# A fused Nystrom attention and squared-ReLU MLP kernel: the softmax A of batches 4 to 7 transposed by DMA instead of TensorE, with a gate on later loads and new instruction orders

## The chip, the cores and the metric

The kernel runs on one core of a Trainium2 chip. The metric is device microseconds of one execution (us). Medians are over the executions of a kernel; "span" is the length of the profiled execution, which is about 2 us shorter than the time reported for it.

## The reference, cut to what matters

```python
# per batch and head, S = 576, D = 64, m = 32 landmarks
A  = softmax(q    @ k_lm.T / 8)        # 576 x 32
Bm = softmax(q_lm @ k_lm.T / 8)        # 32 x 32
C  = softmax(q_lm @ k.T    / 8)        # 32 x 576
Z  = Bm.T / (norm1(Bm) * norminf(Bm) + 1e-6)
for _ in range(6):
    Z = 2 * Z - Z @ Bm @ Z             # the iterated inverse, a serial chain
attn = A @ Z @ C @ v
# then an MLP on 4608 rows: x (4608 x 512), w_in (512 x 2048), w_out (2048 x 512)
out = maximum(x @ w_in, 0) ** 2 @ w_out
```

There are 8 batches of 8 heads. The kernel folds Z @ C @ v @ w_in into a matrix G, so that the MLP's first product is h = G applied to A transposed (AT).

## The kernel before: the parts that matter

The order of instructions on TensorE, VectorE (DVE), ScalarE (ACT) and SyncE (SP) is written out by hand, in strings. `HEAD` orders batch 0's attention. `PLANS[b]` interleaves the MLP of batch b with the attention of batch b+1: `h` is one group of first products (4 matmuls), `s` its squaring on DVE, a number is so many steps of the output product (one 128x512 matmul each), `as`, `ar` are the sums and the scaling of A's rows, `at` its transpose, `gg` a part of G. `LOADS` orders the first loads.

```python
DMA_T = 3      # from this batch on q and k are transposed by DMA
DMA_A = 9      # the same for A: never, there are 8 batches
...
        def a_transposed(i):
            if b >= DMA_A:
                nc.sync.dma_start_transpose(AT[:, i, :]..., an[:, i, :, :]...)
                return
            tps = ntile([P, (NC4 + 1) * P], BF16, placed=b > 0)
            for c in range(NC4 + 1):                       # five 128x128 transposes on TensorE
                nc.tensor.transpose(tps[:, c * P:c * P + P], an[:, i, c, :], ident_bf[:])
            o = TAIL * c0
            return AT[:, i, o:o + S], tps[:, o:o + S]      # then one copy, DVE (i=0) or ACT (i=1)
...
    def mlp_in(b, f, AT, G, gT):
        h = psum.tile([P, 2, 512], F32, tag="h", bufs=2, name="h")
        for qd, j in order:
            nc.tensor.matmul(h[:, j, 0:HALF], lhsT=G[:, qd, f * P:(f + 1) * P],
                             rhs=AT[:, qd, a0 + j * HALF:a0 + (j + 1) * HALF], ...)
        r = mlp.tile([P, S], BF16, tag="r", bufs=3, name="r")
        nc.scalar.activation(r..., h[:, :, 0:HALF], AF.Relu)
        return lambda: nc.vector.tensor_tensor(gT[:, f, o:o + S], r[:], r[:], ALU.mult)
...
                if b > 0 and nm + "turn" in loaded[b - 1]:   # a load waits for the turning
                    tc.add_manual_dep(one.ins, loaded[b - 1][nm + "turn"].ins.name, ...)
```

`w:n:width` in `HEAD` is a filler: n matmuls whose result nobody reads.

The softmax here doesn't subtract the row's maximum and nothing guards it: scores larger than these inputs give would overflow.

Of the kernel before, what the change touches and what calls it, by code (L numbers as in the profile page):

```python
# [9 lines left out]
P = 128  # L10
# [19 lines left out]
HALF = S // 2  # L30
SCALE = 1.0 / 8.0
DMA_T = 3
DMA_A = 9
DMA_C = 9
COMPACT = 1
HEAD = (
    "w:16 ck tk1 mk w:1:256 w:1:256 ek1d w:1:256 w:1 tk0 tt w:1 w:1 cq0 cq1 ek0a mq tq0 tq1 "
    "lm w:1 et w:1:256 w:1 eq0a w:1:256 tl eq1d ls sum:0:4:5 w:1 ib w:1 w:1:256 sq1 w:1:256 "
    "if sk1 sum:1:2:5 w:1:256 w:1 sum:1:0:2 jo w:1:256 w:1:256 rec:1 w:1:256 row:1:0:3 "
    "row:1:3:5 w:1:256 sk0 w:1 sq0 jo w:1:256 w:1:256 w:1 w:1:256 sum:0:2:4 sum:0:0:2 w:1 jo "  # L40
    "rec:0 cv:0 cv:1 w:1:256 w:1:256 row:0:3:5 cr jo w:1:256 row:0:0:3 w:1:256 at:1 cba w:1 "
    "jl at:0 ea0d ea1a ct w:1:256 nu w:1:256 g:0 gl1d fv w:1 gf1d w:1 gf0a az gl0d"
)
LOADS = "w10 v0 w00 q1 w01 w11 o0 o1 o2 o3 v1"
PLANS = [
    (
        "pk h g:1 tt h pq h s tk1 s h s h tq1 s tk0 h h mk s s mq tq0 h lm s g:2 g:3 ls sk0 s h "
        "h ib 1 h 1 s if tl h jo 1 sq0 s 1 jo s s 1 h jo 1 sq1 1 jl h 1 nu h s s h nn 2 sk1 nu s "
        "1 s 8 as0 1 ar0 as1 2 ar1 5 nn1 cv 4 wt at0 2 gg0 2 at1 2 gg1 1"
    ),  # L50
    (
        "2 pk 1 h h 1 mk pq s mq 1 s h tq0 lm h ls h tt tq1 3 tl 1 s 1 h ib 1 s if s sq1 2 s h "
        "jo 1 as1 sq0 1 h h s 1 as0 tk1 1 jo 1 s 4 tk0 2 jo 1 h 1 s h 1 pk+ 1 jl ar1 h sk0 1 s 1 "
        "s nu h s 1 sk1 s h h nn s cv nu h 3 nn1 at1 s 3 s wt 3 ar0 2 gg0 3 at0 1 gg1 pq+"
    ),
    (
        "5 mk h 1 h mq s 2 h 5 lm s 2 ls 1 sk1 2 ib 3 h h s sk0 s if 1 s h 2 h 1 jo s h tl 3 jo "
        "1 s 2 h jo 1 s 2 h 3 s sq0 s 1 jl pk+ 4 sq1 2 as0 nu 3 h 1 nn 2 as1 1 pq+ 1 nu 1 h 1 "
        "ar1 h 1 s s h 1 nn1 cv 1 h 2 ar0 1 s wt h 1 at0 2 gg1 1 s at1 1 s 2 gg0 1 s"
    ),  # L60
    (
        "mk 2 h 1 mq 7 h 2 s lm s 1 ls 1 h sq1 1 h h 1 ib 1 s if sk1 1 s h s 2 h jo 1 s 1 h s 1 "
        "jo 2 h 1 pk+ jo 1 tl s h 2 jl as1 sq0 1 s h 1 s h nu s 1 h sk0 s 1 ar1 4 as0 nn 1 ar0 2 "
        "h 3 cv 2 s h nu 4 s nn1 1 at1 1 h wt 2 s 3 s gg1 1 at0 4 gg0 4 pq+"
    ),
    (
        "2 mk h 2 mq 4 h lm 1 h 1 s ls 1 sk0 s ib s 3 h h if 3 tl s 2 h h s 1 s jo 2 h h 1 jo s "
        "1 sq0 s 2 h 1 jo 5 s 10 jl pk+ s 3 sq1 h nu 1 h 1 h 3 as0 sk1 s 1 h 1 as1 ar1 5 s nn cv "
        "nu pq+ 4 s 2 nn1 ar0 h s 4 wt h 2 at0 s 1 gg0 2 s 1 at1 1 gg1 2"
    ),  # L70
    (
        "3 mk mq 3 h lm 3 h h ls 1 s 1 s ib 2 sq1 h 2 if 1 sq0 3 jo h 1 sk0 s jo 2 s h jo tl 4 "
        "as1 1 h 1 jl s sk1 h 3 pk+ s 4 nu h 1 s 2 s 1 s 4 as0 h 1 ar1 nn s 2 ar0 h cv h nu h s "
        "1 s 1 nn1 h 2 h pq+ s wt h 2 at1 2 gg0 at0 5 s 3 s s gg1"
    ),
    (
        "mk 1 mq 3 h s lm 1 h 3 ls 2 h s 1 ib 2 h 1 if sq1 s h 1 s 3 sq0 2 s h 2 s 2 jo h tl 3 "
        "jo 1 h h as0 jo 3 s h 1 s jl 1 s sk1 4 nu 2 as1 h nn 1 h 1 sk0 2 ar0 nu 1 s s 3 h h 1 "
        "cv 2 nn1 s h s 1 at0 1 wt h 2 s 1 ar1 gg0 1 at1 2 s 1 gg1 4 s"
    ),  # L80
    (
        "h 7 h 6 s 1 h 6 h 1 s 2 h s 2 h 6 s 13 h 2 s 2 h 1 s 1 s 5 s h 3 h 1 s s h 11 s 1 h s 8 "
        "h 1 h 1 h 1 s 4 s h 2 s s"
    ),
]

# [2 lines left out]
def kernel(  # L89
# [9 lines left out]
    nc = tc.nc  # L99
# [27 lines left out]
        nc.vector.memzero(ect[:])  # L127
        ects.append(ect)

    behind, gate = [], []  # L130

    def load(dst, src, queue=nc.gpsimd):
        with tc.issue_after(behind[0].ins) if behind else nullcontext():
            d = queue.dma_start(dst, src)  # L134
        if gate:
            tc.add_manual_dep(
                d.ins, gate.pop().ins.name,
                mybir.DependencyInfo(mybir.DependencyClass.Sync, mybir.DependencyReason.DATA),
                reason="q first")
        if queue is nc.gpsimd:  # L140
            behind[:] = [d]
        return d

    def k_row(b):
        return TAIL if b % 2 == 0 else 0

    def q_row(b):
        return TAIL - k_row(b)
# [12 lines left out]
    def load_qk(b: int, X: dict):  # L161

        X["qkt"] = loads.tile([P, H, D], BF16, tag="qkt", name="qkt")

        def tails():
            for src, r0 in ((k, k_row(b)), (q, q_row(b))):
                load(X["qkt"][r0:r0 + TAIL, :, :],
                     src[b, :, NC4 * P:S, :].rearrange("h p d -> p h d"))

        if b > 0:  # L170
            tails()
        for nm, src in (("k", k), ("q", q)):
            if b < 3:
                X[nm + "raw"] = staged(b, nm)
            else:
                X[nm + "raw"] = loads.tile([P, H, NC4, D], BF16, tag="raw", name="raw")
            parts = ((0, H // 2), (H // 2, H)) if b == 0 and nm == "q" else ((0, H),)
            for lo, hi in parts:
                one = load(
                    X[nm + "raw"][:, lo:hi, :, :],  # L180
                    src[b, lo:hi, 0:NC4 * P, :].rearrange("h (p c) d -> p h c d", c=NC4),
                    nc.sync if b == 0 and nm == "k" else nc.gpsimd)
                if b > 0 and nm + "turn" in loaded[b - 1]:
                    tc.add_manual_dep(
                        one.ins, loaded[b - 1][nm + "turn"].ins.name,
                        mybir.DependencyInfo(mybir.DependencyClass.Sync,
                                             mybir.DependencyReason.DATA),
                        reason="behind the turning of the batch before")
            if b == 0 and nm == "k":
                tails()  # L190

# [10 lines left out]
    loaded = {b: {} for b in range(B)}  # L202
# [31 lines left out]
    for i in range(2):  # L234
        ct = const.tile([P, 2, NC4 + 1, P], BF16, name="ct%d" % i)
# [1 line left out]
        cts.append(ct)  # L237
    nc.vector.tensor_copy(seg[:, NC4 + 2, :], seg[:, NC4, :])

    def load_rest(after):  # L240

        def w_in(i, j):
            load(
                w_in_bf[64 * i:64 * i + 64, :, 1024 * j:1024 * j + 1024],
                moe_w_in[256 * i:256 * i + 256, 1024 * j:1024 * j + 1024].rearrange(
                    "(j d) f -> d j f", d=D),
            )

        def w_out(j):
            load(  # L250
                w_out_bf[:, 4 * j:4 * j + 4, :],
                moe_w_out[512 * j:512 * j + 512, :].rearrange("(ft fp) c -> fp ft c", fp=P),
            )

        behind[:] = [masked]
        for x in LOADS.split():
            i = int(x[1])
            if x[0] == "w":
                w_in(i, int(x[2]))
            elif x[0] == "o":  # L260
                w_out(i)
            else:
                (load_v if x[0] == "v" else load_qk)(i, loaded[i])

    turn = [0]
# [32 lines left out]
    def attention(b: int, R: dict):  # L298

        X = loaded[b]  # L300
        BD = bds[b % 2]
        ect = ects[b % 2]
        first = b == 0
# [193 lines left out]
        ct = cts[b % 2] if b >= DMA_C else None  # L497
        c0 = b % 2
        at = NC4 * (1 - c0)
# [10 lines left out]
        an = attn.tile([P, 2, NC4 + 1, P], BF16, tag="an", bufs=1, name="an")  # L510
        AT = attn.tile([P, 2, (NC4 + 1) * P], BF16, tag="AT", name="AT")
# [55 lines left out]
        one, two = slice(0, 1), slice(1, 2)  # L567
# [20 lines left out]

        def a_transposed(i):
            if b >= DMA_A:  # L590
                nc.sync.dma_start_transpose(AT[:, i, :].rearrange("p (c t) -> p c t", t=P),
                                            an[:, i, :, :].rearrange("p c x -> p (c x)"))
                return
            tps = ntile([P, (NC4 + 1) * P], BF16, placed=b > 0)
            for c in range(NC4 + 1):
                nc.tensor.transpose(tps[:, c * P:c * P + P], an[:, i, c, :], ident_bf[:])  # L596
            o = TAIL * c0
            return AT[:, i, o:o + S], tps[:, o:o + S]
# [42 lines left out]
        act, dve = nc.scalar.copy, nc.vector.tensor_copy  # L641
# [67 lines left out]
        def head_step(token):  # L709
            st = X["state"]  # L710
            name, *args = token.split(":")
            i = int(name[2]) if len(name) > 2 and name[2].isdigit() else 0
            n = [int(x) for x in args if x.isdigit()]
            on = [x for x in args if not x.isdigit()]
            if name == "ck":
                raw = natural(0, "k")
                dve(X["k"][:, 0:2], raw[:, 0:2])
                load_rest(act(X["k"][:, 2:4], raw[:, 2:4]))
                st["qraw"] = natural(0, "q")
                X["tT"] = attn.tile([P, NPAIR, P], BF16, tag="tT", name="tT")  # L720
            elif name[:2] == "cq":
# [62 lines left out]
            elif name == "az":  # L784
                AZ = attn.tile([P, 2, (NC4 + 1) * P], BF16, tag="AT", name="AZ")
                az = [psum.tile([P, 2, 512], F32, tag="h", bufs=2, name="az") for j in range(2)]
# [187 lines left out]
```

## Time and profile before

| | before |
|---|---|
| time, median | 263.62 us (263.31 to 264.01, 4 runs) |
| span | 262.1 us |
| TensorE busy | 254.6 us, 97% of the span |
| first h (start of the MLP) | 23.51 us |
| transposes of A on TensorE | 80 |

The lines that carry this are shown in the prediction below. Two habits of reading are used throughout. First, matmuls overlap in the pipeline, so their durations don't add up to time (a 512-column matmul is recorded with 379 ns on average, but follows the one before it after 216); the chain of work that ended last gives pitches, which do. Second, the end of each batch's plan can be found in that chain: it is marked by the second G group of the plan (plus the few output steps that the plan has behind it), so the time of each plan can be compared between kernels.

### The profile page before, as it was taken

How to read it: one execution, taken by the hardware profiler on the slowest of the kernel's cores; microseconds unless marked ns; L12 is line 12 of the kernel's file. 1: busy time of each engine (PE TensorE's matmuls, PEld its weight loads, DVE VectorE, ACT ScalarE, POOL GpSimd, SP SyncE). 2: the span in 40 equal slices, each digit the busy share in tenths (PEclk: the TensorE clock that was granted, in tenths of full speed). 3: DMA queues.
4: the chain of work that ended last, by engine and by line, in shares of the span. 5: the costliest groups of instructions: out<-in, count | busy, mean ns of one | idle time of the engine just before them, and what ended most of it. 6: DMA issues, size and time to landing. Idle time of an engine off the chain costs nothing.

```text
span 262.1 us, 6993 instructions
## 1 busy us (share of the span) xinstructions
PE 254.6 (97%) x2894; PEld 154.1 (59%) x2894; DVE 176.8 (67%) x488; ACT 158.4 (60%) x278; POOL 45.2 (17%) x70
## 2 busy tenths in 40 slices
PE   7899999999999999999999999999999999999994
PEld 2674765476746655666566565566566655555453
DVE  5798777789985888699757587689776783232000
ACT  1556985478755856687567556775777664364210
POOL 8934234120010503301005010600000000000000
PEclk9999999999999999999999999999999999999999
DMA  8999999999549999995759979699401112112122
GB/s 185 201 194 205 208 205 189 204 210 90 116 48 207 126 173 214 160 170 109 144 103 95 204 149 181 92 197 216 102 22 40 43 43 80 40 44 80 40 80 80
DMA packets 69791, 34.65 MB, mean 132 GB/s; under 512 B 37376, under 2 KB 64256, under 8 KB 69760
## 3 DMA queue, kind: packets, MB, share of 16 engines
q0 software_dynamic: 39808, 17.83, 56.8%
q1 hardware_dynamic: 24704, 7.08, 16.0%
q10 hardware_dynamic: 5248, 9.31, 11.0%
q8 instruction: 22, 0.36, 0.6%
q14 instruction: 9, 0.07, 0.1%
HBM read 36.70 MB, written 9.44 MB: 176 GB/s over the span
## 4 chain that ended last, share of the span: by engine, by line
PE 91%; DVE 4%; DMA 2%; ACT 1%; issue 1%; DVEq 0%
PE ops L851 25%; PE h L822 24%; PE n L851 22%; PE g L805 3%; PE n L530 3%; DMA stage<-in_k_dram 2%; PE n L342 2%; PE n L414 2%; PE n L596 2%; PE idle L295 2%; PE n L614 1%; PE n L313 1%; PE n L629 1%; ACT r L826 1%; PE n L558 1%; DVE gT L827 1%
## 5 line engine op out<-in xcount | busy, mean ns | idle before, releaser
L826 ACT ACTIVATE r<-h 128x576 bf16<-128x576 f32 x128 | 81.3, 652 | 45.9 <-PE h L822 34.1
L851 PE MATMUL ops<-w_out_bf,gT 128*128 128x512 bf16 (+1 forms) x320 | 81.7, 368 | 0.0
L851 PEld LDWEIGHTS <-gT 128*128 128x128 bf16 x592 | 53.2, 98 | 38.7 <-issue 4.2
L851 PE MATMUL n<-w_out_bf,gT 128*128 128x512 bf16 x272 | 74.5, 379 | 0.0
L827 DVE TENSOR_TENSOR gT<-r 128x576 bf16<-128x576 bf16 x128 | 54.9, 448 | 27.2 <-ACT r L826 27.0
L822 PE MATMUL h<-AT,G 128*128 128x288 bf16 x448 | 71.0, 286 | 0.0
L822 PEld LDWEIGHTS <-G 128*128 128x128 bf16 x512 | 47.7, 97 | 24.2 <-ACT AZ L795 0.7
L703 DVE CAST G<-g 128x1024 bf16<-128x1024 f32 x14 | 17.1, 1224 | 5.4 <-PE g L805 5.4
L862 ACT COPY o_sb<-ops 128x512 f32<-128x512 f32 (+1 forms) x19 | 10.9, 574 | 14.5 <-PE ops L851 14.5
L862 ACT COPY o_sb<-n 128x512 f32<-128x512 f32 x17 | 10.0, 587 | 12.9 <-PE n L851 12.8
L703 ACT CAST G<-g 128x1024 bf16<-128x1024 f32 x14 | 14.2, 1015 | 4.5 <-PE g L805 4.5
L295 PE MATMUL idle<-bd 128*128 128x512 bf16 (+1 forms) x51 | 13.3, 377 | 1.5 <-DVE bd L117 1.5
L530 PEld LDWEIGHTS <-T 128*128 128x128 bf16 x256 | 11.3, 98 | 4.2 <-issue 0.6
L134 POOL DMA_DIRECT2D raw<-in_k_dram x5 | 4.5, 891 | 52.2 <-DVE gT L827 25.5
L572 DVE TENSOR_REDUCE ra<-EA 128x20 f32<-128x640 f32 (+3 forms) x19 | 13.2, 703 | 0.3 <-ACT EA L560 0.3
L584 DVE TENSOR_TENSOR an<-EA,rra 128x640 bf16<-128x640 f32 (+2 forms) x18 | 13.2, 737 | 0.2
L530 PE MATMUL n<-bd,T 128*128 128x64 bf16 x256 | 12.7, 193 | 0.0
L535 ACT ACTIVATE EA<-n 128x512 f32<-128x512 f32 x16 | 9.6, 598 | 3.3 <-PE n L530 3.2
L535 ACT ACTIVATE EC<-n 128x512 bf16<-128x512 f32 x16 | 9.5, 596 | 3.0 <-PE n L530 1.6
L134 POOL DMA_DIRECT2D raw<-in_q_dram x5 | 4.4, 884 | 38.2 <-DVE rc L445 17.1
L414 PEld LDWEIGHTS <-ED 128*128 128x128 bf16 x72 | 6.8, 98 | 6.5 <-DVE EY L453 0.9
L822 PE MATMUL h<-AZ,G 128*128 128x288 bf16 x64 | 10.0, 286 | 0.6 <-DVE AZ L795 0.4
(144 smaller groups left out, 287.2 us busy)
## 6 DMA issues: line engine op xcount, KB each, us to landing
out_dram<-o_sb ACTq DMA_DIRECT2D x31, 256.0 KB, 3.4
vm<-in_v_dram POOLq DMA_DIRECT2D x8, 512.0 KB, 10.8
raw<-in_k_dram POOLq DMA_DIRECT2D x5, 512.0 KB, 6.4
raw<-in_q_dram POOLq DMA_DIRECT2D x5, 512.0 KB, 6.2
w_in_bf<-in_moe_w_in_dram POOLq DMA_DIRECT2D x4, 512.0 KB, 12.1
w_out_bf<-in_moe_w_out_dram POOLq DMA_DIRECT2D x4, 512.0 KB, 17.0
out_dram<-o_sb ACTq DMA_DIRECT2D x9, 128.0 KB, 2.4
stage<-in_k_dram SPq DMA_DIRECT2D x1, 1024.0 KB, 5.9
```

The costliest lines, as they stand in the source:

```text
L295: nc.tensor.matmul(idle[:, 0:width], lhsT=z[:, 0:P], rhs=z[:, 0:width], start=True, stop=True)
L414: nc.tensor.matmul(res[a:a + w, qd, :], lhsT=diagonal[a:a + w, qd, :], rhs=moving(qd)[a:a + w], start=True, stop=True)
L530: nc.tensor.matmul(sc[:, c, j, :, :], lhsT=X[nm + "T"][:, c, p, :], rhs=BD[:, 1 if nm == "q" else 0, p, 0:64], start=True, stop=True)
L535: nc.scalar.activation(dst, sc.rearrange("p c j i m -> p c (j i m)"), AF.Exp, scale=SCALE)
L572: nc.vector.reduce_sum(ra[:, quads, lo:hi, :], EA[:, quads, lo:hi, :].rearrange("p q c (h m) -> p q c h m", m=M), axis=AX.X)
L584: on.tensor_tensor(an[:, i, lo:hi, :].rearrange("p c (h m) -> p c h m", m=M), EA[:, i, lo:hi, :].rearrange("p c (h m) -> p c h m", m=M), r ...
L703: (act, dve)[n % 2](G[:, :, n * 512:n * 512 + 512], gg[:])
L822: nc.tensor.matmul(h[:, j, 0:HALF], lhsT=G[:, qd, f * P:(f + 1) * P], rhs=AT[:, qd, a0 + j * HALF:a0 + (j + 1) * HALF], start=(qd == 0), s ...
L826: nc.scalar.activation(r.rearrange("p (j t) -> p j t", j=2), h[:, :, 0:HALF], AF.Relu)
L827: return lambda: nc.vector.tensor_tensor(gT[:, f, o:o + S], r[:], r[:], ALU.mult)
L851: nc.tensor.matmul(ops, lhsT=gT[:, f, t * P:t * P + P], rhs=w_out_bf[:, f, i * n:i * n + n], start=(f == 0), stop=(f == NF - 1))
L862: nc.scalar.copy(o_h, ops)
```

## The change

Its intent: TensorE is the bound, so take the 40 transposes of A of batches 4 to 7 off it and let the DMA engines do them, keep big loads from running beside them, and search anew for orders that suit this. The cut diff leaves out a branch that was never taken and is removed.

```diff
-DMA_A = 9
+DMA_A = 4
 HEAD = ( ... )    # rewritten: 51 fillers become 29, both halves of k transposed before its means
-LOADS = "w10 v0 w00 q1 w01 w11 o0 o1 o2 o3 v1"
+LOADS = "v0 w10 w00 q1 w11 w01 o0 o1 v1 o2 o3"
 PLANS = [ ... ]   # all eight rewritten; batch 0's plan has 12 output steps instead of 38
...
-                if b > 0 and nm + "turn" in loaded[b - 1]:
-                    tc.add_manual_dep(one.ins, loaded[b - 1][nm + "turn"].ins.name, ...)
+                turns = [] if b == 0 else [loaded[b - 1].get(nm + "turn")]
+                if b > 1 and nm == "k":
+                    turns += loaded[b - 2].get("aturn", [])
+                for turn in turns:
+                    if turn is not None:
+                        tc.add_manual_dep(one.ins, turn.ins.name, ...)
...
             if b >= DMA_A:
-                nc.sync.dma_start_transpose(AT..., an...)
+                X.setdefault("aturn", []).append(nc.sync.dma_start_transpose(AT..., an...))
                 return
```

I call the three lines about `aturn` the gate: k of batch 6 is loaded only after A of batch 4 is transposed, k of 7 after A of 5. The loads are issued in order, so q and v behind k wait too.

## The prediction

> **What bounds the kernel now.** I read the shares of the span first, then the chain of work that ended last, then the busy time by stretch, then the groups split by shape.
>
> ```profile
> PE 254.6 (97%) x2894; PEld 154.1 (59%) x2894; DVE 176.8 (67%) x488; ACT 158.4 (60%) x278; POOL 45.2 (17%) x70
> ...
> PE 91%; DVE 4%; DMA 2%; ACT 1%; issue 1%; DVEq 0%
> ```
>
> TensorE is busy for 97% of the span and carries 91% of the chain that ended last; no other engine is above 67%. That busy share alone doesn't say that it runs at its rate, because matmuls overlap. So I take pitches from the chain, where each piece is the time until the next piece begins (columns: start us, length us, what):
>
> ```profile
> 19.63 0.28 PE n L596 x5
> ...
> 208.13 0.98 PE h L822 x8
> ...
> 248.07 3.45 PE n L851 x16
> ```
>
> One 512-column matmul takes 3.45/16 = 0.216 us of the engine, one 288-column matmul 0.98/8 = 0.123, one transpose of a 128x128 block of A 0.28/5 = 0.056, though the groups give means of 379, 286 and 219 ns. With such pitches I add up each batch's plan (16 groups h of 4 x 0.123, so many 512-column steps, the attention pieces of the next batch) and compare it with the distance between the ends of the plans, which the G groups (L805) mark in the chain. For the plans of batches 1 to 6 the sums are 24.9, 27.6, 27.0, 29.3, 26.3 and 26.5 us, the distances 25.4, 27.9, 27.3, 29.7, 27.2 and 26.9. **Only 0.3 to 0.9 us per batch is lost there**: in that part an instruction taken off TensorE is time off the kernel. Two parts lose more, and both are early:
>
> ```profile
> 0.00:24.00 24.00, 20.87 (x324) 12.92 (x324) 17.86 (x59) 10.74 (x21) 16.30 (x33) 1.00 1.26 195
> 24.00:48.00 24.00, 23.64 (x354) 15.03 (x353) 19.19 (x52) 17.45 (x33) 8.49 (x11) 1.00 1.35 201
> ...
> 187.00:213.00 26.00, 26.00 (x305) 15.94 (x303) 19.63 (x59) 17.33 (x31) 0.00 (x0) 1.00 0.17 50
> ```
>
> (columns: length, then busy time of PE, PEld, DVE, ACT, POOL with counts, clock, DMA share, GB/s). The head, from the landing of k at 6.7 to the first h at 23.51, is a serial chain for batch 0 with about 8.4 us of needed TensorE work in the 15.7 us from 7.82; the rest is filler matmuls ("idle", L295) and latency. The plan of batch 0, 23.5 to 51.8 = 28.3 us, has 24.9 us of TensorE work: 3.4 lost, while DVE and ACT are at 80% and 73% in that stretch.
>
> **What the Trainium skill says.** "TensorE: Matmul & The Clock Gate", section Back-to-back issue gap, gives a warm gap of N/2.4 + 2.5 ns for a single stream: 216 ns at 512 columns and 56 at 128. This trace agrees (216, 56). The same section's lower figure for a sustained stream, about 131 ns at 512, this trace does not show. The page's section on the HAM clock gate says that about 3.4 us of idleness halves the clock; the longest idle time of TensorE here is 1.5 us and the granted clock is 1.00, so fewer fillers should not cost clock. "DMA: Bandwidth & Descriptors", section Issuing engines are not separate DMA queues, says that transfers of SP, ACT and POOL share 16 engines and interleave. The trace agrees at least in that a raw load lands after 6.0 us at best and 16.5 at worst. "Perfetto Trace Analysis", section Identifying the Most-Contended Engine, warns of judging by matmul busy time; the 379 against 216 ns above is why I worked with pitches.
>
> **The change part by part.**
>
> 1. Removed: batches 4 to 7 no longer transpose A on TensorE. That is 4 batches x 2 halves x 5 = 40 transposes (80 to 40 in the order of instructions), 8 x 0.28 = **2.24 us of TensorE** on the path.
>
> ```profile
> L596 PE MATMUL n<-ident_bf,an 128*128 128x128 bf16 x80 | 7.1, 219 | 0.0
> ...
> L685 ACT COPY AT<-n 128x576 bf16<-128x576 bf16 x7 | 4.5, 644 | 1.2 <-PE n L596 1.1
> ...
> L685 DVE COPY AT<-n 128x576 bf16<-128x576 bf16 x7 | 3.2, 452 | 0.8 <-PE n L596 0.8
> ```
>
> Four copies of 0.64 us leave ACT (2.6 us) and four of 0.45 leave DVE (1.8 us). Neither is the bound there; I count nothing for it.
>
> 2. Added: 8 transposes by DMA of 128x640, issued from SP. The nearest measured thing is the transpose of the tail tT, 128x512:
>
> ```profile
> L286 SPq DMA_TRANSPOSE tT<-qkt x5: 1188/1244/1552, 54.5 to 161.5; - x5
> ...
> DMA to landing us min/median/max: 4.4/4.4/7.6
> ```
>
> So I estimate 1.4 us of SP each to issue and 4.5 us to land, some 6 us for the two of a batch after the later half of A is written. Is that hidden? From the later of the two row scalings (ar) to the first h that reads AT, I count TensorE pieces in the new plans: 11.6, 11.7, 9.3 and 8.8 us for batches 4 to 7. Take off about 2.3 us for DVE's lag and the 0.8 us scaling: 9.3, 9.4, 7.0 and 6.5 us are left for about 6. **Hidden, but in the last two batches by a hair to 1 us**; there the other DMA traffic is nearly over (50 GB/s in 187 to 213).
>
> 3. The new wait: k of batches 6 and 7 is loaded only after the transposes of A of batches 4 and 5. For batch 6 they land about 0.6 us after the plan of batch 4 begins; k then takes 0.9 to issue and 6.4 to land, q one issue more, so q is there at about 9; its cast stands some 11.5 us into that plan. For batch 7, k is there at about 7 and its cast stands at 9.5. About 2.5 us of slack each: no cost expected. Before, these k loads were issued at 122 and 155 us, long ahead of need.
>
> 4. Moved: the head. 51 fillers become 29 (7 fewer of 512 columns, 15 fewer of 256), and both halves of k are transposed before its means. Up to the softmax of the landmarks I find no gain: Eb has to wait behind a 1.0 us copy on ACT. After that DVE is what the steps of the inverse queue behind:
>
> ```profile
> 15.31 0.88 DVE L572 TENSOR_REDUCE ra<-EA 128x12 f32<-128x384 f32 x2
> 16.11 0.28 DVE L419 SCALAR_TENSOR_TENSOR EY<-EY,n 128x128 bf16<-128x128 bf16 x1
> ...
> 21.77 0.48 DVE L644 TENSOR_SCALAR G<-n,rc 128x256 bf16<-128x256 f32 x1 [0.59 <-PE n L805]
> 22.17 0.21 DVE L419 SCALAR_TENSOR_TENSOR v<-v,n 128x64 bf16<-128x64 bf16 x1
> ```
>
> The new order spreads sums and scalings differently (one sum ahead of the first step, the reciprocal and one sum behind it) and gives the first scaling of G that stood ahead of the last v to ACT. Walking both lists with these durations I get the last v at about 21.4 instead of 22.17 and the first h at about 22.6 instead of 23.51: **0.9 us**.
>
> 5. Moved: the plan of batch 0 now holds 12 output steps instead of 38, so 19.3 us of TensorE work, but its DVE list adds up to about 22 us and its ACT list to 21 at the pitches of the trace. It becomes bound by those two: some 23 us. Before, less the 26 steps moved out (5.6 us), it took 22.7. **Nothing gained, perhaps 0.3 lost.** Later plans get the steps (444 done by the end of batch 6's plan, 418 before) and run at TensorE's rate; from the one idle spot (0.4 us in batch 5's plan, 0.9 lost there) I credit 0.4.
>
> Sum: 2.24 + 0.9 - 0.3 + 0.4 = about 3.3 us, so 263.73 - 3.3 = **260.4 us** (1.3% faster).
>
> **Rivals.** (a) *The transposes or the gated loads come late*, and a wait for them takes the place of the 2.24 us. For it: the worst raw load took 16.5 us, transposes of T up to 8.8, and the DMA slices are at 9 tenths for much of 100 to 190 us. Against: the counts of slack above. It would show as TensorE or DVE idle on AT or raw and give 262 to 265. (b) *DVE and ACT become the bound in batch 0's plan* by more than I counted, since 26 output steps are gone from it and each h needs 0.65 us of ACT against 0.49 of TensorE; two bad us there give 262. (c) *The search found more than I see*: if the head falls to 13.5 us and batch 0's plan to its DVE sum, another 2 us go and 258.4 is reached. Against: the chain of the inverse keeps its steps. (d) *The removed transposes were hidden anyway*: against it, the sums of TensorE match the distances within 0.3 us in most batches.
>
> **Range and chances.** The first term is firm (2.24 us); the early terms are uncertain by about 1 us each, both ways, and rival (a) makes a tail to the slow side. 8 times in 10: 258.7 to 262.2. Faster by over 2% means under 258.5, which needs rival (c): 0.1. Slower by over 2% needs over 5 us of new waits: 0.02. Within 2%: 0.88.
>
> **What would show it.** Transposes at L596 at 40 with TensorE's busy time down; the plans of batches 3 to 6 (which hold the attention of batches 4 to 7) each 0.56 us shorter for the same number of steps; DMA transposes of AT landing in 4 to 6 us with no wait of TensorE for AT; no DVE wait for raw; first h at about 22.6; batch 0's plan about 23 us with DVE and ACT near full. A wait for AT or raw, a first h at 23.5 or later, or a batch 0 plan beyond 25 us would prove me wrong on that step.

## The result, and the profile after

| | before | after |
|---|---|---|
| time, median | 263.62 us (263.31 to 264.01, 4 runs) | 260.91 us (260.31 to 260.98, 4 runs) |
| span | 262.1 us | 258.8 us |
| transposes of A on TensorE | 80 | 40 |
| first h | 23.51 us | 21.99 us |

The ratio is 0.9891 (95% interval 0.9871 to 0.9912), so 1.1% faster, within the 2% that counts as the same.

From the page of the changed kernel (busy time, and the chain that ended last, by engine and line):

```profile
PE 250.1 (97%) x2832; PEld 150.7 (58%) x2832; DVE 174.9 (68%) x483; ACT 156.7 (61%) x275; POOL 45.5 (18%) x70
...
PE 86%; DMA 6%; POOL 4%; DVE 2%; issue 0%; ACT 0%; POOLq 0%; DVEq 0%
PE ops L852 26%; PE h L823 23%; PE n L852 23%; DMA stage<-in_q_dram 6%; PE g L806 3%; PE n L529 3%; PE n L341 2%; PE n L413 1%; PE n L614 1%; POOL qkt L134 1%; PE n L312 1%; PE n L629 1%; POOL stage L134 1%; PE n L596 1%; PE n L557 1%; POOL seg L205 1%
```

TensorE is still the bound, with 4.5 us less of busy time. New is what the 6% of DMA are: the landing of q of batch 1 (before, 2%, the landing of k of batch 0). The groups by shape, and the new transposes with their issues and landings:

```profile
L596 PE MATMUL n<-ident_bf,an 128*128 128x128 bf16 x40 | 3.7, 220 | 0.0
L685 ACT COPY AT<-n 128x576 bf16<-128x576 bf16 x3 | 1.9, 640 | 0.4 <-PE n L596 0.4
...
L685 DVE COPY AT<-n 128x576 bf16<-128x576 bf16 x3 | 1.4, 455 | 0.5 <-PE n L596 0.5
```

```profile
L590 SPq DMA_TRANSPOSE AT<-an x8: 1201/1382/2116, 127.8 to 213.7; - x8
...
DMA to landing us min/median/max: 2.6/3.9/4.7
```

They land in 3.9 us (the median; at most 4.7) and TensorE never waits for them. Now the time of each plan, from the marks in the chains. "Asked" is the difference of output steps times the 0.2156 us of one step; what is left is gained or lost otherwise.

| part | before, us (steps) | after, us (steps) | difference | asked by steps | left |
|---|---|---|---|---|---|
| start to first h | 23.51 | 21.99 | -1.52 | 0 | **-1.52** |
| plan of batch 0 | 28.31 (38) | 23.86 (12) | -4.45 | -5.61 | **+1.16** |
| batch 1 | 25.44 (46) | 29.85 (67) | +4.41 | +4.53 | -0.12 |
| batch 2 | 27.93 (68) | 29.88 (77) | +1.95 | +1.94 | +0.01 |
| batch 3 | 27.34 (65) | 27.81 (70) | +0.47 | +1.08 | **-0.61** |
| batch 4 | 29.68 (76) | 29.91 (79) | +0.23 | +0.65 | **-0.42** |
| batch 5 | 27.20 (62) | 27.17 (67) | -0.03 | +1.08 | **-1.11** |
| batch 6 | 26.87 (63) | 28.25 (72) | +1.38 | +1.94 | **-0.56** |
| batch 7, to the last output step | 42.21 (158) | 36.49 (132) | -5.72 | -5.61 | -0.11 |

The last column sums to -3.3 us, the difference of the spans (3.6 us follow the last output step in both). Plans 3 to 6, which hold the attention of batches 4 to 7, give 2.70 us: the 2.24 of the transposes and about 0.5 more in batch 5's plan, where a small idle time is gone. The head gave 1.5 us, but the plan of batch 0 took 1.2 of it back. Why is seen in two views of the changed kernel. The chain (start, length, what) and DVE's timeline, with what ended its idle time in brackets:

```profile
11.75 14.59 DMA stage<-in_q_dram
26.34 0.02 issue
26.36 0.70 DVE nat L280
```

```profile
23.32 0.69 DVE L280 COPY nat<-stage 128x2048 bf16<-128x2048 bf16 x1 [0.63 <-DMA stage<-in_k_dram]
...
26.36 0.69 DVE L280 COPY nat<-stage 128x2048 bf16<-128x2048 bf16 x1 [0.99 <-DMA stage<-in_q_dram]
```

DVE, ready earlier than before, now stands idle for k and q of batch 1 to land at 23.3 and 26.3 us. Before, it took q up at 25.6 with no wait:

```profile
25.63 0.68 DVE L281 COPY nat<-stage 128x2048 bf16<-128x2048 bf16 x1
```

And by stretches, the columns as in the prediction:

```profile
0.00:24.00 24.00, 20.11 (x318) 11.91 (x318) 17.69 (x60) 12.45 (x25) 16.23 (x33) 1.00 1.26 192
24.00:48.00 24.00, 22.77 (x374) 15.07 (x375) 21.19 (x55) 19.14 (x36) 8.91 (x12) 1.00 1.35 201
```

In 24 to 48 us DVE is now at 88% and ACT at 80%, and TensorE idles 1.2 us.

### The profile page after: what moved, and what is told of

The parts are those of the page before. It is cut to its first block, busy times and chain, and to the rows that moved or that the text cites. A ratio compares the mean times of both kernels' runs of the same rounds, so it can differ in the third digit from the quotient of the medians.

```text
span 258.8 us, 6890 instructions
## 1 busy us (share of the span) xinstructions
PE 250.1 (97%) x2832; PEld 150.7 (58%) x2832; DVE 174.9 (68%) x483; ACT 156.7 (61%) x275; POOL 45.5 (18%) x70
## 4 chain that ended last, share of the span: by engine, by line
PE 86%; DMA 6%; POOL 4%; DVE 2%; issue 0%; ACT 0%; POOLq 0%; DVEq 0%
PE ops L852 26%; PE h L823 23%; PE n L852 23%; DMA stage<-in_q_dram 6%; PE g L806 3%; PE n L529 3%; PE n L341 2%; PE n L413 1%; PE n L614 1%; POOL qkt L134 1%; PE n L312 1%; PE n L629 1%; POOL stage L134 1%; PE n L596 1%; PE n L557 1%; POOL seg L205 1%
## 5 line engine op out<-in xcount | busy, mean ns | idle before, releaser
L852 PE MATMUL n<-w_out_bf,gT 128*128 128x512 bf16 x272 | 72.1, 379 | 0.0
L134 POOL DMA_DIRECT2D raw<-in_k_dram x5 | 4.4, 888 | 80.3 <-DMA AT<-an 23.5
L294 PE MATMUL idle<-bd 128*128 128x512 bf16 (+1 forms) x29 | 9.3, 434 | 1.5 <-DVE bd L117 1.5
L341 PEld LDWEIGHTS <-nat 128*128 128x128 bf16 x256 | 8.2, 96 | 2.7 <-issue 0.5
```

The costliest lines, as they stand in the source:

```text
L134: d = queue.dma_start(dst, src)
L341: nc.tensor.matmul(means[:, ti, p, :], lhsT=src.rearrange("p h d -> p (h d)"), rhs=seg[:, c + (ti if c == NC4 else 0), :], start=(n == 0 a ...
L852: nc.tensor.matmul(ops, lhsT=gT[:, f, t * P:t * P + P], rhs=w_out_bf[:, f, i * n:i * n + n], start=(f == 0), stop=(f == NF - 1))
```

## The experiments

Twelve runs, of eleven kernels, were made, each of five rounds against the kernel before on the same chip; all gave correct results. Medians of the kernel before were 263.16, 263.61 and 263.50 us in the three sessions. Line numbers differ by a few between these kernels.

### What each of the two halves is worth alone

**1. New orders, A transposed on TensorE.**

```diff
 # changed kernel
-DMA_A = 4
+DMA_A = 9
```

> The changed kernel with its new orders and loads, but all of A transposed on TensorE again (and so no gate on k). Theory: the 40 transposes lie on TensorE's path, 8 x 0.28 = 2.24 us, so this takes 260.9 + 2.2 = 263.1 us (262.6 to 263.9, as the last copy of A of batch 7 may now be waited for). Rival, the transposes were hidden and the gain is all from the orders: 260.9 (260.5 to 261.4).

Measured: 264.06 us (262.99 to 265.94, 6 runs), ratio 1.0032 (1.0001 to 1.0062): no faster than the kernel before. (The interval just excludes 1, but three of the six executions, 262.99, 263.04 and 263.65, lie where the kernel before does.) The span of the profiled run is 261.9 us, 3.1 more than after; by the marks 1.47 us of it are in batch 3's plan, 0.71 in 4's, 0.55 in 5's, 0.28 in 6's. So the transposes do lie on TensorE's path (the rival fell), and under these orders they cost more than their 2.24 us. The excess is in batch 3's plan, 1.47 us for ten transposes of 0.56, where the second five wait for the copy of the first five:

```profile
127.49 0.45 PE L596 MATMUL n<-ident_bf,an 128*128 128x128 bf16 x5
127.78 0.38 PE L852 MATMUL n<-w_out_bf,gT 128*128 128x512 bf16 x1
128.62 0.44 PE L596 MATMUL n<-ident_bf,an 128*128 128x128 bf16 x5 [0.46 <-DVE AT L685]
```

The spread of 3 us was not expected; see experiment 11.

**2. Old orders, A transposed by DMA, no gate.**

```diff
 # kernel before
-DMA_A = 9
+DMA_A = 4
```

> The kernel before with its own orders and loads, and A of batches 4 to 7 transposed by DMA (no gate). Theory, the 2.24 us come from the transposes alone and the transfers are hidden under the old orders as well: 263.6 - 2.2 = 261.4 (261.0 to 261.9). Rival, the old orders leave AT no time to land: TensorE waits for AT and the time stays at 262.5 or more.

Measured: 267.24 us (267.10 to 267.93), ratio 1.0155 (1.0139 to 1.0170), slower by 1.6%. The rival holds, and more strongly than I had put it: TensorE waits 3.7 us for AT, 3.1 of it at batch 5's first h, and the granted clock is 0.66 in the 5 us from there on (166 to 171 us).

**3. Old orders with the gate as well.**

```diff
 # the changed kernel's code
-HEAD, LOADS, PLANS of the changed kernel
+HEAD, LOADS, PLANS of the kernel before
```

> The old head, loads and plans with the changed kernel's mechanism: A of batches 4 to 7 by DMA and the gate on k. Without the gate this took 267.2. Theory A, the gate is what makes the transposes land in time, whatever the orders: 261.4 (260.9 to 262.0), no wait of TensorE for AT. Theory B, the old orders issue a transpose too late for the next h even so, or the held k comes late for its cast: 263 or more, with a wait for AT or raw.

Measured: 265.14 us (264.63 to 267.66, 6 runs), ratio 1.0075 (1.0045 to 1.0106). By the two ratios, which are of two sessions, the gate takes back 2 us, but theory B holds. TensorE waits for AT twice: 1.8 us at batch 5's first h and 1.2 at batch 6's. The chain at the first:

```profile
159.62 1.02 ACT G L703
160.65 0.37 SPq L590
161.02 0.05 issue
161.07 5.24 DMA AT<-an
166.31 0.04 issue
166.35 0.42 PE h L823 x2
```

The old plan scales the second half of A at 157.4 us on DVE and wants it in h at 164.1. TensorE's own transposes could be slotted in between; the DMA transpose cannot: SP issues in order, and stands behind the transposes of q of batch 6 until 159.65, so those of A are issued from 159.8 and 161.1 us, and the second lands at 166.3. (The chain puts an issue down to ACT's G; on SP's timeline that issue begins at 159.82, before this G ends.) The new plan has the same transposes issued by 157.5 and its first h at 167.1. The gain therefore belongs to neither half: new orders alone 264.1, DMA alone 267.2 or 265.1, both together 260.6 to 260.9. The 3 us of spread in this run, at clocks of 0.997 to 1.00, are not explained.

### The gate

**4. The changed kernel without the gate.**

```diff
-                if b > 1 and nm == "k":
-                    turns += loaded[b - 2].get("aturn", [])
```

> The changed kernel with DMA transposes, but k of batches 6 and 7 no longer waits for the transposes of A of batches 4 and 5. Theory: the gate costs nothing and buys nothing that TensorE waits for: 260.9 (260.5 to 261.3); the transposes of AT may land later than 4.7 us, beside a raw load. Rival, the gate is needed, as loads slow the transposes until TensorE waits for AT: 262 or more with a wait on AT. Second rival, the gate holds k back in its own right: 260.3 or less.

Measured: 265.97 us (265.11 to 267.90, 6 runs), ratio 1.0115 (1.0081 to 1.0148). My theory fell and the first rival holds. POOL's timeline of this run: the loads of k and q of batch 6 and v of batch 5, issued from 126.4 to 129.8 us.

```profile
126.44 0.89 POOL L134 DMA_DIRECT2D raw<-in_k_dram  x1 [15.40 <-DVE ED L402]
127.31 0.90 POOL L134 DMA_DIRECT2D raw<-in_q_dram  x1
128.18 0.91 POOL L134 DMA_DIRECT2D vm<-in_v_dram  x1
```

SP issues the two transposes of A from 129.4 us on, just behind them. Their landing in this kernel, and what TensorE did:

```profile
DMA to landing us min/median/max: 2.6/4.4/12.6
```

```profile
139.68 0.41 PE L821 MATMUL h<-AT,G 128*128 128x288 bf16 x2 [0.51 <-DMA AT<-an]
143.49 0.64 PE L821 MATMUL h<-AT,G 128*128 128x288 bf16 x2 [3.40 <-DMA AT<-an]
```

A transpose that lands in at most 4.7 us with the gate took 12.6 behind 1.5 MB of loads (the two of batch 4: 10.2 and 12.6). Between the ends of plans 2 and 4 this run lost 5.5 us (64.3 against 58.8): 3.9 of waiting, the rest at a lowered clock after it (0.87 over 135 to 148 us). Another 1.6 us it lost in the head, which is no effect of the gate (experiment 11). In the changed kernel the same k load is issued at 132.9 us, after AT has landed, and no one waits for it; it is the only load that is seen to wait for AT there (23.5 us).

### The head and the first loads

**5. The changed kernel again**, as the measure for experiments 6 and 9.

> The changed kernel unaltered, as the measure for the runs beside it on the same chip. Both theories: 260.9 (260.3 to 261.2). If it shows the wide spread of the run with A on TensorE (263.0 to 265.9), the spread belongs to the thinner fillers of the head and not to that run's edit.

Measured: 260.63 us (260.55 to 260.76), ratio 0.9888 (0.9874 to 0.9903). No wide spread here; the same head shows one in experiments 8 and 10.

**6. The changed kernel with the head of before.**

```diff
-HEAD of the changed kernel
+HEAD of the kernel before
```

> The changed kernel with the head of before (51 fillers, first h at 23.5 in the old trace instead of 22.0). Theory: the chain of batch 1 hangs on the landing of its q (26.3 us), not on the first h, so of the head's 1.5 us only 0.4 us or less reaches the end: 261.3 (260.9 to 261.8). Rival: the head's gain goes through in full: 262.4 (262.0 to 262.9).

Measured: 261.03 us (260.70 to 261.39), ratio 0.9904 (0.9891 to 0.9917). First h is at 23.52 us instead of 21.99, and yet only 0.4 us is lost. The theory holds: DVE takes up q of batch 1 at 26.42 us here, without a wait, and at 26.36 in the changed kernel, after one. The chain runs through the head and the first h here, through q's landing there: all but 0.4 of the head's 1.5 us stop at that landing.

**7. The first loads in the old order**, v of batch 1 still early.

```diff
-LOADS = "v0 w10 w00 q1 w11 w01 o0 o1 v1 o2 o3"
+LOADS = "w10 v0 w00 q1 w01 w11 o0 o1 v1 o2 o3"
```

> The changed kernel with only the first six loads put back to the order of before (w10 v0 w00 q1 w01 w11; v1 stays ahead of o2 and o3). Theory: with the new order the two later quarters of w_in are issued together at 13.1 us and share the engines with q of batch 1, which lands at 26.3 instead of 25.0 us and starts the chain of batch 1 late; put back, q lands at about 25.0, the plan of batch 0 is up to 1.3 us shorter, and the kernel takes 260.0 (259.6 to 260.4). Rival, the plan of batch 0 is bound by the sums of DVE and ACT, whenever q lands: 260.9 (260.6 to 261.3).

Measured: 260.14 us (259.91 to 260.43), ratio 0.9883 (0.9867 to 0.9898), in a session where the kernel before took 263.16. The ratio is within the noise of the changed kernel's 0.9888 and 0.9891, so the time doesn't decide; the profile says more. There q is taken up at 25.45 instead of 26.36 us, and the stretch from first h to the second G group of batch 0's plan is 22.13 instead of 23.22 us, 1.1 of the up to 1.3 that were expected. But first h came at 22.53 instead of 21.99 (22.27 in the profiles of experiments 1 and 5, which have the new load order and the same head), so part of it was lost in the head. And q no longer sets the pace: DVE takes it up without a wait, and the chain runs through the first h.

```profile
25.45 0.69 DVE L280 COPY nat<-stage 128x2048 bf16<-128x2048 bf16 x1
```

From first h to that G group it is 22.1 us in each profile with the clock at 1.00 and either the old load order (experiments 7, 9 and the second of 10) or the old head (experiment 6); with the new head and the new load order it is 23.2, 22.7 and 22.7 (changed kernel, experiments 1 and 5). So the wait for batch 1's loads comes on top of some 22.1 us that stay. Of these DVE is busy 91% and ACT 85% in this run, so rival and theory each hold in part; no experiment shows that DVE and ACT are what the 22.1 us consist of.

**8. The same kernel once more.**

> The same kernel as the run with the six early loads in the old order, once more, beside the two that follow on one chip. If q of batch 1 sets the pace of batch 0's plan: 260.0 (0.6 to 0.9 under the changed kernel's 260.6 to 260.9). If the changed head loses as much as batch 0's plan gains: 260.5, within 0.3 of the changed kernel.

Measured: 259.50, 259.95, 260.50 in three executions, 262.49, 262.63 and 262.64 in three others; median 261.49, ratio 0.9915 (0.9876 to 0.9954). The faster three stand some 0.7 us below the changed kernel, the slower three show something else (experiment 11). What the old load order is worth in the time stays unresolved. In the profiles with the clock at 1.00 the second G group of batch 0's plan begins at 44.3 to 44.6 us with it (experiments 7, 9 and the second of 10, on TensorE's timeline), and at 45.0 to 45.1 with the new one (changed kernel, experiments 1 and 5): about half a microsecond.

### More batches

**9. Old load order, and A of batches 3 to 7 by DMA.**

```diff
-DMA_A = 4
+DMA_A = 3
-LOADS = "v0 w10 w00 q1 w11 w01 o0 o1 v1 o2 o3"
+LOADS = "w10 v0 w00 q1 w01 w11 o0 o1 v1 o2 o3"
```

> The changed kernel with the early loads in the old order (260.1 on its chip) and the A of batch 3 by DMA as well (k of batch 5 then waits for it). Theory: ten more transposes, 0.56 us, leave TensorE and the transfer is hidden: 259.6 (259.2 to 260.0). Rival: DMA is busier there, AT of batch 3 or k of batch 5 comes late: 260.5 or more with a wait for AT or raw.

Measured: 259.69 us (259.48 to 260.01, 4 runs), ratio 0.9854 (0.9841 to 0.9867), against 260.63 for the changed kernel beside it. This is the best version found, and it beats both kernels on that chip. From the end of plan 1 to that of plan 3 it takes 57.35 us against 57.69: of the 0.56 us that left TensorE 0.34 were gained. Another 0.64 us are gained by the second G group of batch 0's plan already (44.34 against 44.98 us on TensorE's timeline), so by the load order. No wait for AT or raw on TensorE.

**10. The two edits apart, and one batch further.** First A of batch 3 by DMA with the changed kernel's own loads:

> The changed kernel with its own loads and only the A of batch 3 by DMA as well. Theory: ten transposes, 0.56 us, and no more: 0.9888 of before less 0.0021, so 0.9867, about 260.1. Rival, the 0.9 us of the earlier run with both edits came from the loads: 260.6.

Measured: 260.80 us (260.29 to 262.53, 6 runs), ratio 0.9893 (0.9876 to 0.9909). Its profiled execution fell on the slow head of experiment 11. From the end of plan 1 to that of plan 6 it takes 142.25 us, the changed kernel 142.58 in experiment 5 and experiment 9 142.25: the third of a microsecond is there, though the time hides it. The theory's 260.1 was missed: without the slow execution the median is still 260.77, nearer the rival's 260.6, so most of experiment 9's gain belongs to the loads. Then A of batches 2 to 7 by DMA:

> The changed kernel with early loads in the old order and the A of batches 2 to 7 by DMA. Counting TensorE pieces from the later scaling of batch 2's A to its first h gives 7.6 us, less 2.3 of lag leaves 5.3 us for a landing of about 6. Theory: TensorE waits for AT of batch 2 by about 1 us and what is gained on transposes (0.56) is lost: 260.0 or more, above the 259.7 of batch 3 to 7. Rival, the count has slack: 259.1.

Measured: 261.39 us (259.10 to 262.83, 6 runs), ratio 0.9913 (0.9876 to 0.9951); the spread forbids a verdict by time. The profile, which is of an undisturbed head, decides it: from the second G group of batch 0's plan to that of batch 6's it takes 172.86 us against 172.50 in experiment 7 (twenty transposes more) and 172.17 in experiment 9 (ten more), so fewer transposes and more time. The theory holds, with a smaller wait than I had put:

```profile
76.97 0.41 PE L823 MATMUL h<-AT,G 128*128 128x288 bf16 x2 [0.46 <-DMA AT<-an]
```

Here the gate costs something too: k of batch 4, held until AT of batch 2 is there, goes out at 77.58 us and takes 8.2 to land. DVE stands idle 1.9 us for it, TensorE 0.2 behind DVE, and the chain runs through this load.

### The fillers

**11. The changed kernel without the 13 fillers inside the head's chain.**

```diff
 HEAD = (
-    "w:16 ck tk1 tk0 ek0a w:1 ek1d w:1:256 cq0 w:1 mk cq1 w:1 tt mq et tq0 ...
+    "w:16 ck tk1 tk0 ek0a ek1d cq0 mk cq1 tt mq et tq0 ...      # all later w: gone too
```

> The changed kernel with its 13 fillers inside the head's chain left out (the 16 at the start stay). Theory: they keep the granted clock of TensorE up through the thin head; without them it falls to about half in the stretch from 16 to 26 us in most executions, as it did in the profile of the run without the gate (0.52 in 20 to 24), and the kernel takes 262 or more, with a spread over 1 us. Rival, they only take up slots: 260.6 or less, clock 1.00 throughout.

Measured: 261.75 us (260.96 to 263.60, 6 runs), ratio 0.9940 (0.9913 to 0.9968), slower than the changed kernel by half a per cent, though the head has less to do. In the profiled execution (columns as above, the clock third from the end):

```profile
12.00:16.00 4.00, 2.89 (x64) 2.06 (x61) 3.83 (x17) 3.41 (x8) 1.93 (x4) 1.00 1.22 209
16.00:20.00 4.00, 3.52 (x101) 2.29 (x101) 3.57 (x13) 1.48 (x5) 1.53 (x3) 0.74 1.53 189
20.00:24.00 4.00, 3.58 (x42) 1.92 (x36) 2.98 (x7) 2.30 (x5) 2.15 (x3) 0.50 1.44 203
```

So the fillers hold the clock, and without them it halves; the mean clock of all six executions is 0.978 to 0.987. The theory holds on the clock and the spread; the time is a little under its 262. The 29 that are left hold it only most of the time. The same stretch in the second run of experiment 8's kernel and in experiment 10's first kernel:

```profile
16.00:20.00 4.00, 3.05 (x95) 1.93 (x95) 3.25 (x13) 1.38 (x4) 1.44 (x3) 1.00 1.53 186
20.00:24.00 4.00, 3.67 (x48) 1.54 (x47) 2.64 (x9) 2.12 (x6) 2.22 (x3) 0.52 1.42 202
```

```profile
16.00:20.00 4.00, 2.44 (x84) 1.57 (x82) 2.65 (x11) 0.78 (x4) 0.87 (x2) 1.00 1.44 193
20.00:24.00 4.00, 3.67 (x56) 1.53 (x49) 2.59 (x8) 2.07 (x6) 2.31 (x3) 0.54 1.48 199
```

Both have the changed kernel's head, unaltered. The second G group of batch 0's plan is at 47.04 and 47.28 us, against 44.66 (experiment 7) and 45.21 (changed kernel) with the clock at 1.00: some 2 us. In these two TensorE was busy 3.05 and 2.44 of the 4 us before the fall, and 2.96 in experiment 4's, which fell too (to 0.52); in six profiles of this head without a fall it was 3.07 to 3.44, in four with the old head 3.86 to 4.00. The difference begins at one spot, where TensorE idles in the middle of the row sums of C, and for which the profile shows no reason:

```profile
18.51 0.24 PE L629 MATMUL n<-ones_bf,EC 128*128 128x1 bf16 x4 [1.31 <-issue]
```

In the changed kernel's profile that gap is 0.31 us, at 17.40. It is 0.31 to 0.52 us in the six profiles without a fall and 0.70, 0.78 and 1.31 in the three with one; that it brings the fall about is not tested. The Trainium skill, "TensorE: Matmul & The Clock Gate", section Part 1: The HAM clock gate, says that the monitor's window of about 3.4 us runs freely, so that the same kernel meets it at another phase each time; a spread from run to run in one kernel agrees with that, but no run here shows the phase. What makes the gap short or long is open. That the slow executions of experiments 1, 8 and 10 that were not profiled have the same cause is likely from their 2 us, not shown.

## Why the prediction was right, point by point

**The sum.** Predicted 260.4 us, measured 260.91; the span of the profiled execution fell by 3.3 us, just the sum of the terms, the median time by 2.7. But two terms were off and cancelled, which was luck.

**Step 1, the transposes:** 2.24 us on TensorE's path. Confirmed by the plans of batches 3 to 6, which gained 2.70 us together with the 0.4 that was credited separately for batch 5's idle spot, and by experiment 1, where putting them back cost at least that much. Rival (d), that they were hidden, is out. (The prediction's argument against it, sums within 0.3 us of the distances in most batches, misreads its own list: that is so in two batches of six, the rest lie 0.4 to 0.9 apart.)

**Step 2, the DMA transposes hidden:** right; I had put 4.5 us for a landing, it was 3.9. The fear for the last two batches was unfounded, as 2.6 to 4.7 us leaves more than I had.

**Step 3, the gate:** right in that no one waits for the gated loads (k of batch 6 went out at 132.9 us; I had it about there). What I missed is its worth. I looked only at what it could cost; experiment 4 shows that without it rival (a) comes true, by 5 us. The landing time that I took from the tail's transpose holds only because the gate keeps the 1.5 MB of loads out of the way.

**Step 4, the head:** the mechanism was right, the size not: first h at 21.99 us (22.27 in experiment 5's profile of the same kernel) instead of 22.6, a gain of 1.2 to 1.5 where I had 0.9. The last v came at 20.73 where the walk through the lists had 21.4; 0.26 us is k's landing, 6.46 against 6.72.

**Step 5, batch 0's plan:** the size was off the other way, +1.16 us where I had put 0.3. I had it bound by the sums of DVE and ACT, some 23 us. That is about what is left where nobody waits for q: 22.1 us to the second G group, 22.8 to the plan's end in experiment 7. What I missed is the wait that comes on top in the changed kernel, for the landing of batch 1's k and q: the chain runs through q's landing (through k's in experiment 5), moving first h by 1.5 us moved the end by 0.4, and bringing q 0.9 us earlier shortened the plan by 1.1. The prediction doesn't speak of the load order; with the new one q lands at 26.3 us, with the old one at 24.7 (kernel before) and 25.2 (experiment 7).

**The clock.** I had argued from the longest idle time, 1.5 us, that fewer fillers would cost no clock. The four executions of the changed kernel and four more in experiment 5 bear that out in the time; the same head in experiments 4, 8 and 10 does not. It was luck to that extent.

## What to carry to other kernels

An operation moved from the busiest engine to DMA pays only if its result is wanted late enough, so the order around it has to move too: here neither half of the change alone made the kernel faster. Keep bulk loads out of the way of a small transfer that someone waits for; a gate that costs nothing on its own was worth 5 us. And before thinning fillers or shortening a head, look at what the next stage hangs on, and at how busy TensorE stays.

## What the Trainium skill lacked or had wrong

- "DMA: Bandwidth & Descriptors" says that the queues' transfers share the engines, but has no time to land for a DMA transpose from SBUF to SBUF, alone or beside loads (only bandwidths): 128x640 bf16 landed in 2.6 to 4.7 us (median 3.9) with the loads held back, and in up to 12.6 us behind three 0.5 MB loads.
- "TensorE: Matmul & The Clock Gate", section Back-to-back issue gap: the sustained 131 ns for 512 columns and 81 ns for 128 in a stream of weight loads and matmuls is not seen; here 216 and 56 ns, the page's isolated formula, held with a weight load ahead of every matmul.
- The same page's section on the HAM clock gate, and its rules for kernels, give figures for idle gaps over about 3 us only; another section, on psum-queue depth-cycling, says that frequent short idling can make the clock go up and down too, without a figure. Here the clock fell to 0.50 to 0.54 with no idle gap over 1.3 us in the 4 us before (0.4 at most in experiment 11's kernel), with TensorE busy 2.44 to 3.05 us of these 4; in the profiles with 3.07 and more it held. With two neighbours so close, this is no threshold.
- No page has the idle time of TensorE without a visible cause in the head: 0.31 to 1.31 us at the same instruction in different profiles of the same head.
